# A transformer block on one core: another schedule for the row maxima of its softmax

## The chip, the cores and the metric

The kernel runs on 1 core of one Trainium2 chip. The metric is device time in microseconds (us) per execution, the median of several runs.

The engines are named as the profile names them: PE (TensorE; PEld is its weight load), DVE (VectorE), ACT (ScalarE), POOL (GpSimd), SP (SyncE, which here mostly issues DMAs).

## The reference

One transformer block with adaptive LayerNorm over a sequence of S = 2048 rows and D = 448 columns, 16 heads of 28, F = 1792:

```python
mod = (_silu(c) @ w_mod).reshape(c.shape[0], 6, 1, -1)
sa, ca, ga, sb, cb, gb = (mod[:, 0], mod[:, 1], mod[:, 2], mod[:, 3], mod[:, 4], mod[:, 5])
h = _layernorm(x, axis=-1) * (1 + ca) + sa
x = x + ga * _A_ref(h, A_wqkv, A_wo)             # softmax attention, 16 heads
h = _layernorm(x, axis=-1) * (1 + cb) + sb
x = x + gb * _B_ref(h, B_w1, B_b1, B_w2, B_b2)   # LayerNorm, dense, gelu, dense
```

In the attention, `p = _softmax(scores)` over 2048 keys for each of 16 x 2048 query rows, `o = p @ v`, and the heads' outputs times `wo`. The change touches the softmax alone.

## The kernel before

Matmuls that need precision are split in a high and a low part in a one-pass format (hi·hi + lo·hi + hi·lo, the "three terms"). The program has three stages: projections to queries, keys and values; the attention loop; the MLP.

**The attention loop.** Heads lie four to a group g (four groups), 32 partitions apart, so a group fills 128 partitions. Queries are cut in four blocks qt of 512. One *unit* u is one (g, qt), 16 units; one *step* is 128 keys of a unit, 16 steps kt per unit, 256 in all. A step makes, for two *halves* hf of two heads each, the scores [128 keys, 2 heads, 512 queries] by 3 terms x 2 matmuls into a two-bank tile in PSUM, then ACT's exponential of the whole tile (L1167). Behind both halves stands the product with V of the step before (L1132, `av`), which fills all 128 rows of the PE array, where a score matmul fills 28 or 29. Row sums come out of a column of ones in V.

**The row maxima.** The exponential needs the row maximum subtracted. It is taken from the high parts alone, ahead of time: for a unit (g, qt), each of 4 chunks cch of 512 keys, 4 row blocks i and 4 heads j, one matmul [128 queries, 512 keys] (`max_mm`, L466) into a one-bank tile, and one DVE reduction of 512 to 1 (`max_one`, L471): 64 per unit, 1024 in all. When a unit's 64 are counted, `max_fin` reduces and transposes them, and small DMAs put them into the query tile `qst` as a further row, so that the score matmul subtracts them. The maxima of unit u+1 must therefore be done before its first step. `mxq` is the queue of maxima that may be made; `emit_max` takes one from it, `finish_max` forces the rest of a unit.

In the projection stage some maxima are made in *pairs* already (`pair_diff`): with k1 - k0 as key, ACT's relu of the scores' difference, then DVE adds q·k0 to it and takes the maximum in one operation (L483), since max(a, b) = a + relu(b - a).

Of the 1024 maxima 884 single ones are made in the loop or near it: four in an even step, three in an odd one, until they run out in unit 14 (`n_maxima`).

**Tiles in PSUM.** Eight banks: two score tiles `s0`, `s1` of two banks, a bank `o` for the product with V, and three banks for maxima (`m1`, and `m2` with two buffers). When no maxima are left, `third_tile` closes `m2` and opens a third score tile `s2` in its place. A tile is written again only when its last reader is done.

**Other work in the loop.** `sched` holds functions by step: the end of a unit (`unit_end_tasks`: denominators by DMA, reciprocal on DVE, product on POOL, a cast on DVE), the output projection (`t_wo`, steps 8 to 11 of units 12 to 15, "projection steps", with `load_o` as its loads), the second LayerNorm of block 0 (`ln2_stages`), weight preparation. The order of every engine's instructions is that in which the code emits them.

Of the kernel before, what the change touches and what calls it, by code (L numbers as in the profile page):

```python
# [27 lines left out]
NB = S // 512  # L28
# [4 lines left out]
P1RATE = 4  # L33
YTAGS = [f"{a}{i}" for a in ("kh", "qh") for i in range(4)]
# [5 lines left out]
def tile_adaln_block(ctx: ExitStack, tc: tile.TileContext, x, wqkv, wo, w1, b1, w2, b2, c, w_mod, out):  # L40
# [42 lines left out]
    def slot4(tag, inner, dt=F32R):  # L83
        if tag not in halved:
            t = slot(tag, [128, 4] + inner, dt)
            return lambda k: t[:, k]
        t2 = [slot(tag + h, [128, 2] + inner, dt) for h in ("", "h")]
        return lambda k: t2[k // 2][:, k % 2]

    def ps_s2():  # L90
        s_ring.append(s_ring.pop(0))
        key = s_ring[-1]
        return ps_pools[key][1].tile([128, 2, 512], F32, tag=key, name=nm(key), bufs=1)
# [365 lines left out]
    def max_mm(g, qt, i, j, k, ps=None):  # L459
        if (g, qt) not in mxp:  # L460
            mxp[(g, qt)] = sbt("mxp", [128, 4, 4, 4], bufs=6)
            if (g, qt) in paired:
                pool.memset(mxp[(g, qt)][:, :, :, 0:1], -3.0e38)
# [25 lines left out]

    def load_hi(kind, g, b):  # L490
        tg = ("kh" if kind else "qh") + str(b)
        t = sb.tile([128, 512], F32R, tag=tg, name=nm(tg), bufs=1)
        (kh_sb if kind else qh_sb)[(g, b)] = t
        sp.dma_start(f(t), f(dscr[kind][0][g])[:, b * 512 : (b + 1) * 512])

# [67 lines left out]
    last_j = [None]  # L563

    def emit_max(n, half=None):
        for _ in range(n):
            if not mxq:
                return
            fits = [x for x, m in enumerate(mxq[:32]) if half is None or (m[4] // 2 == half and m[4] != last_j[0])]
            g, qt, cch, i, j = mxq.pop(fits[0] if fits else 0)  # L570
            last_j[0] = j
            max_one(g, qt, cch, i, j)
            count(g, qt, [cch])

# [35 lines left out]
    def finish_max(g, qt):  # L610
        while left[(g, qt)] > 0:
# [185 lines left out]
    s_ring[:] = ["s1", "s0"]  # L797
    mx_ring[:] = ["m1", "m2", "m2"]

    def third_tile(on):  # L800
        ps_close("m2" if on else "s2")
        ps_open("s2" if on else "m2", "right")
        s_ring[:] = s_ring + ["s2"] if on else ["s1", "s0"]
        mx_ring[:] = ["m1"] if on else ["m1", "m2", "m2"]

    phase1[0] = False
    for item in deferred:
# [63 lines left out]
    def unit_end_tasks(u, o_sb):  # L871
# [62 lines left out]
        if len(parts) > 1 and not staged:  # L934
            tasks.append((0, lambda: load_o(qt)))
# [136 lines left out]

    for i in range(5):
# [7 lines left out]
    for i in range(14):  # L1081
        at(last0 - 12 + i, lambda i=i: lnst[0][0](i))
    for k in range(NC):
        at(last0 + 3 + k, lambda k=k: lnst[0][1](k))
# [23 lines left out]
    plain = [0]  # L1108
# [6 lines left out]
    def left_steps(s_):  # L1115
        rest = range(s_, NKT * (NU - 1) - 6)
        n_wo = sum(is_wo(x) for x in rest)
        return len(rest) - n_wo, n_wo


    def n_maxima(s_):
        n_plain, n_wo = left_steps(s_)
        over = len(mxq) - 7 * n_plain // 2
# [173 lines left out]
```

## Time and profile before

| | |
|---|---|
| median of 3 runs | 1128.31 us (1128.06 to 1128.99) |
| the profiled execution | 1130.08 us, span 1128.0 us |
| granted PE clock | 1.0 of full speed |
| the attention loop, from the first exponential of step 0 to that of step 255 | 170.26 to 830.90 us |
| busy: PE, DVE, ACT, POOL | 1116.4, 843.7, 672.0, 209.6 us |
| DVE's maxima in the loop (L471 from `m`) | 884, 568.8 us, 686 ns each |
| exponentials (L1167), 512 | 1019 to 1025 ns each |

The profile is of one execution on this core. The timeline gives start and duration of instructions on each engine, in brackets the idle time before one and what released it; consecutive like ones are merged with a count. The windows give busy time and counts of instructions in a stretch, the groups the mean duration by line and shape. Matmuls are pipelined, and four of them on different rows of the array can run at once, so the sum of their durations is larger than the time that passes.

### The profile page before, as it was taken

What the parts mean: (1) busy time and instruction counts of PE and PEld (TensorE: products, weight loads), DVE (VectorE), ACT (ScalarE), POOL (GpSimd) and SP (SyncE); (2) the same over time, 40 slices, a digit from 0 to 9 for tenths busy, and PEclk for the clock granted to TensorE, in tenths of its full rate; (3) what the DMA queues carried; (4) which work ended last, traced back from release to release, by engine and by line L of the source; (5) the groups of instructions that cost most, each with busy time, mean ns of one, the idle gap of its engine ahead of it and who ended that gap; (6) DMA issues with size and microseconds to landing.
All of it is one profiled execution on the core that took longest, in us unless ns stands there. A gap on an engine that the chain in (4) does not pass through costs nothing.

```text
span 1128.0 us, 20665 instructions
## 1 busy us (share of the span) xinstructions
PE 1116.4 (99%) x8319; PEld 670.1 (59%) x8319; DVE 843.7 (75%) x1485; ACT 672.0 (60%) x823; POOL 209.6 (19%) x211
## 2 busy tenths in 40 slices
PE   8999999999999999999999999999999999999998
PEld 6756674444444444444444454545468888888887
DVE  6968788999999999999999978595448853444322
ACT  4555657888887888788788867576752321111110
POOL 1533332110000000000000020217114504123000
PEclk9999999999999999999999999999999999999999
DMA  9562263121121211311111312020422100000000
GB/s 303 202 200 88 91 200 114 48 84 41 58 95 57 58 40 57 91 53 58 53 44 58 112 41 83 4 85 1 137 73 78 35 33 1 1 33 1 33 1 33
DMA packets 49341, 81.19 MB, mean 72 GB/s; under 512 B 12311, under 2 KB 18702, under 8 KB 49234
## 3 DMA queue, kind: packets, MB, share of 16 engines
q1 hardware_dynamic: 48762, 79.14, 22.1%
q8 instruction: 65, 1.06, 0.4%
q10 hardware_dynamic: 148, 0.46, 0.1%
q0 software_dynamic: 336, 0.28, 0.1%
q14 instruction: 30, 0.25, 0.1%
HBM read 55.04 MB, written 26.48 MB: 72 GB/s over the span
## 4 chain that ended last, share of the span: by engine, by line
PE 94%; DVE 3%; ACT 1%; DMA 1%; issue 1%; POOL 0%; SPq 0%; DVEq 0%; ACTq 0%; POOLq 0%
PE s L1162 26%; PE o L1132 22%; PE m L386 16%; PE pa L386 8%; PE m L466 6%; PE s L1232 3%; PE s L1233 3%; PE s L1231 3%; DVE mxp L471 2%; PE t L1232 1%; PE t L1233 1%; PE t L1231 1%; DMA slot_c<-in_w_mod_dram 1%; PE ma L466 1%; PE o L267 1%
## 5 line engine op out<-in xcount | busy, mean ns | idle before, releaser
L471 DVE TENSOR_REDUCE mxp<-m 128x1 f32<-128x512 f32 x884 | 568.8, 686 | 75.3 <-PE m L466 41.1
L1162 PE MATMUL s<-slot_b,slot_a 28*128 28x512 f32 (+1 forms) x3072 | 376.3, 420 | 0.0
L1162 PEld LDWEIGHTS s<-slot_b,slot_a 28*128 28x128 f32 (+1 forms) x3072 | 213.0, 184 | 247.4 <-ACT slot_c L1167 124.1
L466 PE MATMUL m<-kh,qh 28*128 28x512 f32 x863 | 287.6, 472 | 1.2 <-DVE mxp L471 0.9
L1167 ACT ACTIVATE slot_c<-s 128x1024 f32<-128x1024 f32 x170 | 174.3, 1025 | 75.9 <-PE s L1162 75.6
L1132 PE MATMUL o<-slot_c,v 128*32 128x512 f32 x680 | 178.8, 605 | 0.0
L1208 ACT ACTIVATE full<-m,b_col 128x512 f32<-128x512 f32 x56 | 38.6, 689 | 192.0 <-PE m L386 175.5
L1132 PE MATMUL o<-slot_c1h,v 128*32 128x512 f32 x512 | 134.7, 605 | 0.0
L1132 PE MATMUL o<-slot_c0h,v 128*32 128x512 f32 x512 | 134.7, 605 | 0.0
L1167 ACT ACTIVATE slot_c0h<-s 128x1024 f32<-128x1024 f32 x128 | 130.4, 1019 | 2.4 <-PE m L386 2.4
L1167 ACT ACTIVATE slot_c1h<-s 128x1024 f32<-128x1024 f32 x128 | 130.4, 1019 | 0.0
L1211 DVE CAST hi<-full 128x512 fp32r<-128x512 f32 x56 | 25.5, 455 | 134.6 <-ACT full L1208 134.6
L466 PEld LDWEIGHTS m<-kh,qh 28*128 28x128 f32 x863 | 114.3, 182 | 8.6 <-DVE mxp L471 5.1
L1167 ACT ACTIVATE slot_d<-s 128x1024 f32<-128x1024 f32 x86 | 88.1, 1025 | 39.3 <-PE s L1162 39.1
L895 POOL TENSOR_TENSOR osb<-osb,osb 128x512 f32<-128x512 f32 x16 | 20.9, 1307 | 441.1 <-DMA osb<-drec 356.8
L1132 PE MATMUL o<-slot_d,v 128*32 128x512 f32 x344 | 90.5, 605 | 0.4 <-ACT osb L1101 0.4
L386 PE MATMUL m<-y,slot_a 128*128 128x512 f32 x160 | 60.7, 395 | 0.0
L1132 PEld LDWEIGHTS o<-slot_c,v 128*32 128x32 f32 x680 | 24.5, 108 | 52.4 <-issue 49.5
L1212 DVE TENSOR_TENSOR lo<-full,hi 128x512 fp32r<-128x512 f32 x56 | 44.2, 788 | 5.9 <-DVE hi L1211 0.9
L471 DVE TENSOR_REDUCE mxp<-ma 128x1 f32<-128x512 f32 x54 | 35.6, 683 | 7.1 <-PE m L466 4.8
L386 PE MATMUL m<-y,slot_v 128*128 128x512 f32 x112 | 39.2, 396 | 0.0
L386 PE MATMUL m<-y,slot_b 128*128 128x512 f32 x112 | 39.0, 398 | 0.0
(316 smaller groups left out, 1626.7 us busy)
## 6 DMA issues: line engine op xcount, KB each, us to landing
slot_b<-d SPq DMA_DIRECT2D x32, 256.0 KB
slot_a<-d SPq DMA_DIRECT2D x32, 256.0 KB
d<-lo SPq DMA_DIRECT2D x28, 256.0 KB
d<-hi SPq DMA_DIRECT2D x16, 256.0 KB
osb<-drec SPq DMA_DIRECT2D x15, 256.0 KB
out_dram<-xn SPq DMA_DIRECT2D x16, 224.0 KB
raw<-in_B_w_dram SPq DMA_DIRECT2D x14, 224.0 KB
qh<-d SPq DMA_DIRECT2D x12, 256.0 KB
```

What stands on the lines that cost most here:

```text
L386: pe.matmul(p, a, b, start=(i == 0), stop=(i == len(terms) - 1))
L466: pe.matmul(m, qh_sb[(g, qt)][js, i * 128 : (i + 1) * 128], k[js, :], start=True, stop=True)
L471: dve.tensor_reduce(out=mxp[(g, qt)][:, i, j, cch : cch + 1], in_=m, op=ALU.max, axis=AX.X)
L1132: pe.matmul(o[32 * j : 32 * j + 32, :], v_sb[kt // 4][:, kt % 4, 4 * g + j, :], p[j // 2][:, j % 2, :], start=(kt == 0), stop=(kt == NKT - 1),
L1162: pe.matmul(s2[:, jj, :], ks[rows_, kp, kc], qs[rows_, qp, :], start=(term == 0), stop=(term == 2))
L1167: act.activation(pt[hf], s2, AF.Exp, scale=SCALE)
L1208: act.activation(gf, p, AF.Gelu_apprx_tanh, bias=b1_col[:, i : i + 1])
L1211: dve.tensor_copy(ghi, gf)
L1212: dve.tensor_tensor(out=glo, in0=gf, in1=f(ghi), op=ALU.subtract)
L1231: pe.matmul(pp, ghi[:, ts], w_hi, start=(m == 0), stop=False)
L1232: pe.matmul(pp, ghi[:, ts], w_lo, start=False, stop=False)
L1233: pe.matmul(pp, glo[:, ts], w_hi, start=False, stop=(m == NFT - 1))
```

## The change

Three things are changed in the order of the maxima, and a few tasks are moved.

1. Up to step 118 one pair of maxima every two steps is made in two steps, as in the projection stage. `make_kd` has POOL subtract two key chunks; at the end of an odd step, behind the product with V, `open_pair` emits the max matmul of the difference and ACT's relu; in the next odd step `close_pair` emits the second matmul and DVE's add-and-max in the place of one single maximum. An odd step so covers four maxima with three DVE operations.
2. From step 119 (`RING`), outside the projection steps, three score tiles are open (`s0`, `s1`, `s2`) and one bank `m1` for maxima. A step's first half is in `s0`, its second half in `s1` or `s2` by turns, and the third tile holds two maxima of neighbouring heads, which one DVE reduction of 2 x 512 to 2 takes (`emit_pair`); a single one goes to `m1`. Three maxima per step, with one more where `extra` finds it due. The half that comes first alternates by step.
3. In projection steps three maxima are made, in the old tiles.

Moved: the queries of the next unit are loaded in step 4 instead of 1, `load_o` four steps earlier, the second LayerNorm of block 0 three steps later, `finish_max` from step 10 to 12 of a unit. The maxima of all units are first set to a low value on POOL.

The counts of the built program: in the loop before, 884 single reductions; now 564 single ones, 55 pairs by relu and 105 wide reductions (564 + 110 + 210 = 884). Up to step 118 every step covers four maxima but a few (none in steps 28 and 29); from step 119 to 234 every step makes three, `extra` is never used, and the last maxima stand in step 235, before in step 233.

The diff, cut to what the text speaks of:

```diff
+LAST_MAX = NKT - 4
+RING = 119
+PAIR_AT = (2, 2, 0, 2)
+WO_MAX = 3
...
+def make_kd(g):
+    c0 = PAIR_AT[g]
+    kd.update(g=g, t=slot("d0h", [128, 1, 512]), **{"from": clock[0] + 1})
+    pool.tensor_tensor(out=kd["t"][:, 0, :], in0=f(kh_sb[(g, c0 + 1)]), in1=f(kh_sb[(g, c0)]), op=ALU.subtract)
...
+def open_pair():
...
+            p = max_mm(g, qt, i, j, kd["t"][:, 0, :])
+            r = slot("d0i", [128, 1, 512], F32)[:, 0, :]
+            act.activation(r, p, AF.Relu)
+            px_open.append((m, r))
...
+def close_pair():
+    (g, qt, cch, i, j), r = px_open.pop()
+    p = max_mm(g, qt, i, j, kh_sb[(g, cch)])
+    dve.tensor_tensor_reduce(
+        out=r, in0=p, in1=r, scale=1.0, scalar=-3.0e38, op0=ALU.add, op1=ALU.max,
+        accum_out=mxp[(g, qt)][:, i, j, cch + 1 : cch + 2],
+    )
+    count(g, qt, [cch, cch + 1])
...
+def emit_pair(half, t):
...
+            for jj in range(2):
+                max_mm(g, qt, i, j + jj, kh_sb[(g, cch)], lambda: t[:, jj])
+            dve.tensor_reduce(out=mxp[(g, qt)][:, i, j : j + 2, cch], in_=t, op=ALU.max, axis=AX.X)
...
-            if kt == 1 and u + 1 < NU and u + 1 not in qst:
+            if kt == 4 and u + 1 < NU and u + 1 not in qst:
                 load_q(u + 1)
-            if kt == NKT - 6 and u + 1 < NU:
+            clock[0] = step
+            if kt == LAST_MAX and u + 1 < NU:
                 finish_max(*divmod(u + 1, NB))
...
-            n = n_maxima(step)
-            n0 = 1 if n == 3 and step % 4 == 3 else 2
+            now[0] = turns[step % 2]
+            first = step % 2 if step >= RING else 0
+            pt = {hf: slot(tags[step % len(tags)], [128, 2, 512], F32) for hf, tags in zip((first, 1 - first), ptags)}
+            was, ring = ring, step >= RING and (three or not is_wo(step))
+            if ring != was:
+                third_tile(ring)
+            more = ring and not three and extra(step)
+            late_one, after = after, more
+            n_max = 0 if ring else WO_MAX if is_wo(step) else 4 - step % 2
+            n0 = 1 if step % 4 == 3 else 2
+            closing = bool(px_open) and step % 2 == 1
...
-            for hf in range(2):
-                s2 = ps_s2()
+            for n, hf in enumerate((first, 1 - first)):
+                s2 = ps_s2() if three else ps_two((now[0] if n else "s0") if ring else ("s0", "s1")[n])
                 for term, (kp, qp) in enumerate(((0, 0), (1, 0), (0, 1))):
+                    if ring and n == 1 and term == 2 and mxq:
+                        emit_pair(first, ps_two(turns[1 - step % 2]))
                     for jj in range(2):
                         rows_ = slice(64 * hf + 32 * jj, 64 * hf + 32 * jj + DH + (term == 0))
                         pe.matmul(s2[:, jj, :], ks[rows_, kp, kc], qs[rows_, qp, :], start=(term == 0), stop=(term == 2))
-                    if hf == 0 and term < min(n0, n):
-                        emit_max(1, 1)
-                    if hf == 1 and term == 2 and n > n0:
-                        emit_max(n - n0, 0)
+                    if closing:
+                        if (n, term) == (0, 0):
+                            close_pair()
+                    elif n == 0 and term < n0 <= n_max:
+                        emit_single(1, ps_mx)
+                    if n == 1 and term == 2:
+                        for _ in range(2 if closing else n_max - n0):
+                            emit_single(0, ps_mx)
+                    if ring and (n, term) == ((1, 0) if late_one else (0, 0)) and not three:
+                        emit_single(1 - first, ps_mx)
+                    if n == 1 and term == 2 and more:
+                        emit_single(first, ps_mx)
                 act.activation(pt[hf], s2, AF.Exp, scale=SCALE)
...
+            if step % 2 and step + 2 < RING:
+                open_pair()
```

How the order of instructions moves is seen best in single steps. PE, step 182 of the loop (unit 11, step 6), before: score matmuls L1162 into `s1` and `s0`, maxima L466 into the `m` tiles, the product with V L1132 into `o`.

```order
L1162 MATMUL s1_2022_8436<-slot_b1_1846_7704,slot_a1_1500_6273 128x512 x2
L466 MATMUL m2_2023_8439<-kh0_1717_7166,qh1_1522_6358 128x512
L1162 MATMUL s1_2022_8436<-slot_b1_1846_7704,slot_a1_1500_6273 128x512 x2
L466 MATMUL m2_2024_8444<-kh1_1757_7331,qh1_1522_6358 128x512
L1162 MATMUL s1_2022_8436<-slot_b1_1846_7704,slot_a1_1500_6273 128x512 x2
L1162 MATMUL s0_2025_8450<-slot_b1_1846_7704,slot_a1_1500_6273 128x512 x6
L466 MATMUL m1_2026_8457<-kh1_1757_7331,qh1_1522_6358 128x512
L466 MATMUL m2_2027_8460<-kh1_1757_7331,qh1_1522_6358 128x512
L1132 MATMUL o_1975_8250<-slot_c0_2011_8398,v1_229 32x512 x2
L1132 MATMUL o_1975_8250<-slot_c1h_2012_8399,v1_229 32x512 x2
```

The same step in the changed program, where score matmuls are L1287, maxima L474 and the product L1245:

```order
L1287 MATMUL s0_2034_8434<-slot_b1_1908_7862,slot_a1_1606_6486 128x512 x2
L474 MATMUL m1_2035_8437<-kh2_1797_7352,qh1_1634_6608 128x512
L1287 MATMUL s0_2034_8434<-slot_b1_1908_7862,slot_a1_1606_6486 128x512 x4
L1287 MATMUL s1_2036_8445<-slot_b1_1908_7862,slot_a1_1606_6486 128x512 x4
L474 MATMUL s2_2037_8450<-kh1_1757_7171,qh1_1634_6608 128x512 x2
L1287 MATMUL s1_2036_8445<-slot_b1_1908_7862,slot_a1_1606_6486 128x512 x2
L1245 MATMUL o_1995_8267<-slot_c1h_2025_8399,v1_230 32x512 x2
L1245 MATMUL o_1995_8267<-slot_c0_2024_8398,v1_230 32x512 x2
```

Four maxima have become three, two of them in one two-bank tile `s2`, ahead of the last two score matmuls; in step 183 `s1` and `s2` change places.

ACT in steps 86 to 88, before: the exponentials alone.

```order
L1167 ACTIVATE slot_c1_1220_5100<-s1_1222_5102 128x1024
L1167 ACTIVATE slot_c0h_1221_5101<-s0_1228_5123 128x1024
L1167 ACTIVATE slot_d0_1231_5141<-s1_1233_5143 128x1024
L1167 ACTIVATE slot_c1h_1232_5142<-s0_1235_5154 128x1024
L1167 ACTIVATE slot_c0_1238_5172<-s1_1240_5174 128x1024
L1167 ACTIVATE slot_c0h_1239_5173<-s0_1243_5188 128x1024
```

The same steps in the changed program, with the exponentials at L1300 and the relu at L631:

```order
L1300 ACTIVATE slot_c1_1295_5246<-s0_1297_5248 128x1024
L1300 ACTIVATE slot_c0h_1296_5247<-s1_1300_5262 128x1024
L1300 ACTIVATE slot_d0_1303_5280<-s0_1305_5282 128x1024
L1300 ACTIVATE slot_c1h_1304_5281<-s1_1307_5293 128x1024
L631 ACTIVATE slot_d0i_1311_5313<-m1_1310_5311 128x512
L1300 ACTIVATE slot_c0_1312_5315<-s0_1314_5317 128x1024
L1300 ACTIVATE slot_c0h_1313_5316<-s1_1317_5331 128x1024
```

The relu of tile `m1_1310` stands between the odd step's second exponential and the even step's first one.

More of the change, by code (lines that the diff above doesn't have):

```diff
@@ L796, in tile_adaln_block @@
         ps_open(key)
[L797 to L798 removed]
+    turns = ("s1", "s2")
     def third_tile(on):
@@ L1107, in tile_adaln_block @@
     o = None
-    plain = [0]
+    due = [0.0]
+    now = [None]
     three = False
@@ L1137, in tile_adaln_block @@
     ptags = (["d0", "c0", "c1"], ["c0h", "c1h"])
-    done_max = set()
+    after = False
+    ring = False
     for u in range(NU):
```

128 lines of the change are left out of this document (101 added, 27 removed).

## The prediction

> **What bounds the kernel now.** I read first the page's engine rows, then one stretch of the attention loop by engine, then two steps of it instruction by instruction, and last the groups for durations.
>
> ```profile
> PE 1116.4 (99%) x8319; PEld 670.1 (59%) x8319; DVE 843.7 (75%) x1485; ACT 672.0 (60%) x823; POOL 209.6 (19%) x211
> ```
>
> PE is called 99% busy, but a busy PE may be waiting in the middle of its pipeline, so this row decides nothing. The windows of the exponentials (two per step) give the pace; the columns are length, busy time and count:
>
> ```profile
> 212.60:464.82 252.22, 199.75 (x206) 1.00 0.20 62
> 464.82:643.07 178.25, 141.59 (x146) 1.00 0.21 64
> 779.19:787.14 7.95, 7.65 (x8) 1.00 0.01 2
> 212.60:464.82 252.22, 252.22 (x2428) 112.90 (x2428) 236.61 (x389) 203.64 (x213) 16.80 (x19) 1.00 0.20 62
> ```
>
> Steps 16 to 118 take 252.22 / 103 = 2.449 us each, steps 119 to 191 178.25 / 73 = 2.442. The third row is steps 236 to 239, where no maxima are left and a third score tile is open: 1.99 each. The fourth row is all engines over the first window (PE, PEld, DVE, ACT, POOL): DVE is busy 236.61 / 51.5 = 4.59 us of every two steps of 4.89, so it is close, but not full. What sets 4.89 shows in the timeline of two steps, an even one with four maxima and an odd one with three (start, duration):
>
> ```profile
> 402.12 1.02 ACT L1167 ACTIVATE slot_c1h<-s 128x1024 f32<-128x1024 f32 x1
> 403.36 1.02 ACT L1167 ACTIVATE slot_c<-s 128x1024 f32<-128x1024 f32 x1 [0.23 <-PE s L1162]
> 404.28 1.02 ACT L1167 ACTIVATE slot_c0h<-s 128x1024 f32<-128x1024 f32 x1
> 406.09 1.02 ACT L1167 ACTIVATE slot_c<-s 128x1024 f32<-128x1024 f32 x1 [0.80 <-PE s L1162]
> 407.01 1.02 ACT L1167 ACTIVATE slot_c1h<-s 128x1024 f32<-128x1024 f32 x1
> ```
>
> ```profile
> 402.35 0.50 PE L1162 MATMUL s<-slot_b,slot_a 29*128 29x512 f32 x2
> 402.69 0.99 PE L1162 MATMUL s<-slot_b,slot_a 28*128 28x512 f32 x6
> 403.18 0.18 PEld L1162 LDWEIGHTS s<-slot_b,slot_a 29*128 29x128 f32 x2 [0.31 <-ACT slot_c1h L1167]
> 403.21 0.50 PE L466 MATMUL m<-kh,qh 28*128 28x512 f32 x1
> 403.52 0.39 PE L1162 MATMUL s<-slot_b,slot_a 28*128 28x512 f32 x2
> 403.75 0.40 PE L1162 MATMUL s<-slot_b,slot_a 28*128 28x512 f32 x2
> 404.09 0.62 PE L1132 MATMUL o<-slot_d,v 128*32 128x512 f32 x2
> 405.09 0.50 PE L1162 MATMUL s<-slot_b,slot_a 29*128 29x512 f32 x2
> 405.35 0.74 PE L1162 MATMUL s<-slot_b,slot_a 29*128 29x512 f32 x8
> 405.89 0.40 PE L466 MATMUL m<-kh,qh 28*128 28x512 f32 x2
> 406.25 0.62 PE L1132 MATMUL o<-slot_c,v 128*32 128x512 f32 x2
> 407.25 0.50 PE L1162 MATMUL s<-slot_b,slot_a 29*128 29x512 f32 x2
> 402.93 4.76 DVE L471 TENSOR_REDUCE mxp<-m 128x1 f32<-128x512 f32 x7 [0.28 <-PE m L466]
> ```
>
> Read it as a ring of waits. The odd step's second exponential starts at 402.12 and ends at 403.14. Only then is its score tile free, and the even step's second half loads weights at 403.18 (0.31 of waiting, released by ACT). From there 0.91 to the product with V at 404.09, 1.00 to the odd step's first score at 405.09, 1.00 to its first exponential at 406.09, 0.92 to its second at 407.01: 407.01 - 402.12 = 4.89, the period. No maximum is on this ring. Two score tiles set it, and maxima ride along as long as DVE's 4.59 fits.
>
> **The change, part by part.** Durations that the terms use:
>
> ```profile
> L471 DVE TENSOR_REDUCE mxp<-m 128x1 f32<-128x512 f32 x884 | 568.8, 686 | 75.3 <-PE m L466 41.1 <-PE ma L466 8.4 <-PE s L1162 4.2
> L502 DVE TENSOR_REDUCE m<-mxp 128x16 fp32r<-128x64 f32 x16 | 3.5, 220 | 0.6
> L1167 ACT ACTIVATE slot_c1h<-s 128x1024 f32<-128x1024 f32 x128 | 130.4, 1019 | 0.0
> L479 ACT ACTIVATE slot_d0h<-m 128x512 f32<-128x512 f32 x23 | 13.3, 597 | 20.4 <-PE m L466 11.5 <-PE ma L466 7.6 <-PE o L466 1.4
> L483 DVE CUSTOM_DVE_ANT_0 slot_d0h<-m,slot_d0h 128x512 f32<-128x512 f32 x8 | 5.5, 682 | 0.0
> L483 DVE DVE_READ_ACCUMULATOR2_ANT mxp<- 128x1 f32 x39 | 3.2, 83 | 0.0
> L905 DVE CAST hi<-osb 128x512 fp32r<-128x512 f32 x15 | 6.3, 417 | 3.7 <-POOL osb L895 3.7
> L886 DVE RECIPROCAL den<-den 128x16 f32<-128x16 f32 x16 | 3.9, 244 | 4.3 <-DMA den<-osb 4.3
> L509 DVE STREAM_TRANSPOSE full<-m 128x32 f32<-128x32 f32 x16 | 3.2, 203 | 0.1
> L429 POOL TENSOR_TENSOR lo<-full,hi 128x512 fp32r<-128x512 f32 x16 | 20.6, 1286 | 33.2 <-ACT hi L425 15.3 <-issue 12.5 <-DVE hi L425 4.0
> ```
>
> *Three score tiles, step 119 on, 105 plain steps.* The ring above is cut: a step's second half no longer waits for the exponential of the step before, but for the wide reduce, which read that tile. Count from a step's first score. The single reduce starts 0.58 later (402.93 - 402.35) and takes 0.69: 1.27. The wide matmuls can start at 0.80 (405.89 - 405.09) and end 0.40 later, so the wide reduce starts at 1.27, behind the single one. Its duration no row shows: 448 more elements cost 686 - 220 = 466 ns, 1.04 ns each, so 512 more make it 1.22. From below, ACT's step from 512 to 1024 (597 to 1019) adds 0.42: 1.11; from above, twice the narrow one: 1.37. I take 1.22, from the same engine and operation. Then 1.27 + 1.22 = 2.49, 0.04 to the waiting second half, 0.91 to the product, 1.00 to the step after next: 4.44 for two steps, 2.22 each. Behind the waiting score stand the wide matmuls of that step and the product with V, so all of PE waits. The floor is the odd step of today, 407.25 - 405.09 = 2.16: it holds the same PE work, twelve score matmuls and three maxima, with no wait. By the bounds of the wide reduce a step takes 2.16 to 2.30; ACT needs about 2 x 0.92 plus a tail and fits. Term: 105 x (2.442 - 2.22) = -23.3, bounds -29.6 to -14.9.
>
> This needs PE to start the second half's scores while the first half's still run. In the rows it does: the odd step's next scores start at 405.35, 0.26 after the first, and the maximum at 403.21 starts ahead of scores at 403.52 that stand before it in program order. The Trainium skill, page "PSUM — Partial Sum Buffer", section "Engine vs sequencer instructions", says that matmuls start and complete in program order; by that rule the ring step would be no shorter than today's. The trace disagrees here (403.21 before 403.52), so it stays a rival with a small chance.
>
> *The pair by relu, 55 times up to step 118.* Each adds a max matmul behind the product in the odd step, a relu on ACT, and 0.083 of accumulator read; the fused add-and-max (682 ns) takes the place of a reduce (686). DVE's seven operations per two steps now cover eight maxima; the ones saved let the later stage run at three per step. The relu waits for its matmul, which starts with the even step, and both exponentials of that step queue behind it. New ring: matmul 0.50, relu 0.50 (597 less the 0.10 by which exponentials overlap, 1.02 against 0.92), exponentials 0.92 + 1.02, 0.04 to PE, 0.91 to the product, 1.00 to the next even step: 4.89, as long as the old one, with nothing to spare. DVE beside it: 4.59 + 0.08 = 4.67 by today's overlap; without overlap 7 x 0.686 + 0.083 + a unit's other work (417 + 244 + 220 + 203 = 1.08 us in 8 pairs of steps, 0.14) = 5.02. So 0 to +0.13; I take +0.08, nearer DVE's end, since two full rings must now hold at once. A gain is excluded, since the ring of two score tiles stays. From above, if the relu lies on the ring whole: +0.60. Term: 55 x 0.08 = +4.4, likely bounds 0 to +7.2. Two steps without any maxima (28, 29) gain nothing for the same reason.
>
> *Moved work.* Query loads three steps later, output loads four steps earlier (two to six DMAs on SP's queue, which still have 12 steps or 24 us), block 0's second LayerNorm three steps later, and on POOL whole memsets and four subtracts of 1.29: POOL is busy 16.80 of 252.22. The last unit's maxima end at step 235 instead of 233, still ahead of that unit's start at 240, about 8 us at 1.99 a step. Opening and closing the third tile around the projection steps may cost a few tenths, six times; the LayerNorm's shift may give as much. All taken as 0, bounds -2.6 to +3. If SP's or POOL's cover fails, one unit waits once for some 1.3 to 3 us. Projection steps keep their three maxima.
>
> Sum: -23.3 + 4.4 + 0 = -18.9. Against the profiled execution's 1130.08 (span 1128.0) that is 1111.2; the median of the timed runs, 1128.31, is 1.8 lower, and the sum is taken from it: **1109.4**.
>
> **The rivals.**
>
> *A, PE's floor.* The wide reduce is cheap, the relu free: -29.6, so 1098.7. For: DVE's reduces partly overlap today. Against: the relu's ring is as long as 4.89, and DVE's end longer.
>
> *B, DVE paces both stages.* The wide reduce costs 1.37 (a step of 2.30) and unit-end work lands between the reduces, 1.08 in 16 steps, half of it felt: 2.33, so 105 x 0.112 = -11.8; pairs at 5.02, +7.2: -4.6, 1123.7. For: DVE at 94% in the windows. Against: in the ring stage it needs 0.69 + 1.22 = 1.91 of 2.22. With a little more of each this reaches no change.
>
> *C, slower: the relu on the ring whole.* ACT is in order, and the tile that the relu reads comes free only after it; the third maximum behind it waits for that tile, then the product. If both exponentials of the odd step shift by 0.60, pairs cost 5.49: 55 x 0.60 = +33.0, with -23.3 it is +9.7, 1138.0. It turns the sign where a pair of steps costs over 4.89 + 23.3 / 55 = 5.31. Against: ACT waits 0.23 and 0.80 in a pair of steps, more than the relu's 0.50.
>
> *D, slower: strict order on PE.* The ring's second half starts only after the first's third score, 0.34 + 0.23 = 0.57 in (402.69 - 402.35, 403.75 - 403.52), then 0.91 and 1.00: 2.48 per step, 105 x 0.04 = +4.0, with +4.4: 1136.7. Against: the rows named above. Such an order is what the Trainium skill states, page "PSUM — Partial Sum Buffer", section "Engine vs sequencer instructions".
>
> **How the numbers follow.** Forecast 0.62 (its own range 1100 to 1121), A 0.06, B 0.17, C 0.11, D 0.04. About 0.2%, 2.3 us, is what a measurement of this kernel can tell from no change. Faster: 0.62 + 0.06 + 0.12 of B = 0.80; within: the other 0.05 of B; slower: C and D, 0.15. The range takes in the forecast and B with small additions, 1100 to 1126, and leaves out A, C and D, 0.21.
>
> **What would show it.** In the profile after: exponentials in the ring stage 2.2 us per pair, score weights in their second half waiting for DVE and not for ACT; wide reduces of 1.22; steps 16 to 118 at 2.45 to 2.52 each, relus of 0.6 ahead of the even step's exponentials. The forecast is wrong if ring steps stay above 2.35, if even and odd step before step 119 take over 5.1 together, or if PE's scores of a step no longer overlap.

## The result, and the profile after

The changed kernel takes **1126.53 us** (median of 20 runs, 1124.64 to 1128.93) against 1128.64 for the kernel before (20 runs): a ratio of 0.9978, 95% interval 0.9972 to 0.9984. It is faster by 2.1 us, where 18.9 were forecast and the range ended at 1126. The profiled execution took 1128.93 (span 1127.2), the longest of the 20 and 2.4 above their median; that of the kernel before was 1.4 above its own. So the stages below, read from the two traces, add up to -0.8 and not to -2.1.

The engine rows of the page and the groups of the three kinds of maxima (partitions x elements and count, then busy time and mean ns of one, then the idle time before them):

```profile
PE 1113.3 (99%) x8319; PEld 675.3 (60%) x8319; DVE 803.6 (71%) x1380; ACT 695.2 (62%) x878; POOL 216.5 (19%) x228
L479 DVE TENSOR_REDUCE mxp<-m 128x1 f32<-128x512 f32 x564 | 364.2, 685 | 97.7 <-PE m L474 68.0
L674 DVE TENSOR_REDUCE mxp<-s 128x2 f32<-128x1024 f32 x105 | 128.6, 1225 | 4.2 <-PE s L474 0.2
L638 DVE CUSTOM_DVE_ANT_0 slot_d0i<-m,slot_d0i 128x512 f32<-128x512 f32 x55 | 38.0, 690 | 15.7 <-PE m L474 11.4
```

The wide reduce takes 1225 ns, as estimated (1.22), and DVE does 40 us less. The windows of the exponentials over steps 0 to 118 in the kernel before (its steps 119 to 191 stand in the prediction), and over steps 0 to 118 and 119 to 191 in the changed one:

```profile
170.26:464.82 294.56, 230.88 (x238) 1.00 0.21 64
```

```profile
174.14:481.24 307.10, 231.28 (x239) 1.00 0.20 60
481.24:646.44 165.20, 141.87 (x146) 1.00 0.26 76
```

The borders and lengths give an account by stage (us):

| stage | before | after | difference | forecast |
|---|---|---|---|---|
| up to the loop's first exponential | 170.3 | 174.1 | +3.9 | 0 |
| steps 0 to 118 (pairs) | 294.6 | 307.1 | +12.5 | +4.4 |
| steps 119 to 191 (three tiles) | 178.3 | 165.2 | -13.0 | -16.2 |
| steps 192 to 239 (32 plain ones) | 144.1 | 141.2 | -2.9 | -7.1 |
| from step 240 on | 340.8 | 339.5 | -1.3 | 0 |

Four stages are over the forecast: the one before the loop, the pairs, the three tiles, and the steps from 192 on with the projection steps. Their causes were read from the trace and then tried by experiment. The -1.3 of the last stage lies in unit 15 up to step 255 (43.8 us before, 42.5 after); its cause was not tried.

**Before the loop** a memset is waited for. POOL, then DVE, of the changed kernel (start, duration, in brackets the idle time before and what ended it):

```profile
31.25 1.29 POOL L438 TENSOR_TENSOR lo<-full,kh 128x512 fp32r<-128x512 f32 x1
32.50 1.29 POOL L438 TENSOR_TENSOR lo<-full,raw 128x512 fp32r<-128x512 f32 x1
33.72 0.16 POOL L471 MEMSET mxp<- 128x64 f32 x1
```

```profile
33.91 1.29 DVE L479 TENSOR_REDUCE mxp<-ma 128x1 f32<-128x512 f32 x2 [3.76 <-POOL mxp L471]
```

In the changed kernel the tile that receives the first maxima is set low first. The memset takes 0.16, but it is issued with the first max matmul, behind POOL's splits, so the first reduce waits 3.76 and holds the PSUM tile that TensorE needs next.

**In unit 12** (steps 199 and 200) there is a stall of 3.04 + 7.05 us where the steps around take 2.3 to 4.4. SyncE's issues, POOL and DVE of the changed kernel there:

```profile
652.79 0.32 SPq L996 DMA_DIRECT2D drec<-den  x1
655.48 0.54 SPq L998 DMA_DIRECT2D osb<-drec  x1
656.07 0.94 SPq L760 DMA_DIRECT2D slot_b<-d  x2
```

```profile
662.15 1.28 POOL L1003 TENSOR_TENSOR osb<-osb,osb 128x512 f32<-128x512 f32 x1 [25.80 <-DMA osb<-drec]
```

```profile
663.46 0.43 DVE L1013 CAST hi<-osb 128x512 fp32r<-128x512 f32 x1 [2.02 <-POOL osb L1003]
663.80 0.68 DVE L479 TENSOR_REDUCE mxp<-m 128x1 f32<-128x512 f32 x1
```

The small `osb` load issued at 655.48 lands at 662, with the moved query load right behind it. DVE stands at the cast of that unit, with the maxima behind it in its queue, and TensorE waits for those. Behind this wait the granted clock of this execution fell, as these windows show (PE, PEld, DVE, ACT, POOL, then clock, DMA share and GB/s):

```profile
664.00:668.00 4.00, 3.07 (x21) 0.98 (x21) 3.50 (x5) 2.27 (x3) 1.24 (x1) 0.79 0.03 6
668.00:672.00 4.00, 4.00 (x28) 2.91 (x24) 0.10 (x1) 0.53 (x1) 0.14 (x1) 0.78 0.00 0
```

Over step 200 it is 0.76, so some 1.7 of its 7.05 us (0.24 x 7.05) are the slower clock.

### The profile page after: what moved, and what is told of

Same layout as the page of the kernel before. It is cut to its first block, busy times and chain, and to the rows that moved or that the text cites. A ratio compares the mean times of both kernels' runs of the same rounds, so it can differ in the third digit from the quotient of the medians.

```text
span 1127.2 us, 20699 instructions
## 1 busy us (share of the span) xinstructions
PE 1113.3 (99%) x8319; PEld 675.3 (60%) x8319; DVE 803.6 (71%) x1380; ACT 695.2 (62%) x878; POOL 216.5 (19%) x228
## 4 chain that ended last, share of the span: by engine, by line
PE 86%; DVE 2%; ACT 1%; DMA 1%; issue 1%; POOL 0%; SPq 0%; DVEq 0%; POOLq 0%; ACTq 0%
PE s L1287 21%; PE o L1245 21%; PE m L395 16%; PE m L474 7%; PE pa L395 5%; PE s L1367 3%; PE s L1368 3%; PE s L1366 3%; PE s L474 1%; PE t L1367 1%; PE t L1368 1%; PE t L1366 1%; DVE mxp L479 1%; DMA osb<-drec 1%; PE m L276 1%
## 5 line engine op out<-in xcount | busy, mean ns | idle before, releaser
L479 DVE TENSOR_REDUCE mxp<-m 128x1 f32<-128x512 f32 x564 | 364.2, 685 | 97.7 <-PE m L474 68.0
L1287 PE MATMUL s<-slot_b,slot_a 28*128 28x512 f32 (+1 forms) x3072 | 355.3, 424 | 1.7 <-DVE mxp L674 0.8
L1287 PEld LDWEIGHTS s<-slot_b,slot_a 28*128 28x128 f32 (+1 forms) x3072 | 211.1, 183 | 172.0 <-ACT slot_c L1300 93.3
L474 PE MATMUL m<-kh,qh 28*128 28x512 f32 x598 | 221.0, 462 | 2.3 <-DVE mxp L479 0.6
L1300 ACT ACTIVATE slot_c<-s 128x1024 f32<-128x1024 f32 x170 | 174.6, 1027 | 55.7 <-PE s L1287 52.4
L1245 PE MATMUL o<-slot_c,v 128*32 128x512 f32 x680 | 179.7, 607 | 0.0
L1245 PE MATMUL o<-slot_c1h,v 128*32 128x512 f32 x512 | 135.5, 608 | 0.9 <-ACT slot_c1h L1300 0.9
L1245 PE MATMUL o<-slot_c0h,v 128*32 128x512 f32 x512 | 134.7, 605 | 0.0
L1300 ACT ACTIVATE slot_c0h<-s 128x1024 f32<-128x1024 f32 x128 | 131.3, 1026 | 3.3 <-PE m L395 2.4
L674 DVE TENSOR_REDUCE mxp<-s 128x2 f32<-128x1024 f32 x105 | 128.6, 1225 | 4.2 <-PE s L474 0.2
L1300 ACT ACTIVATE slot_c1h<-s 128x1024 f32<-128x1024 f32 x128 | 130.7, 1021 | 0.0
L1300 ACT ACTIVATE slot_d<-s 128x1024 f32<-128x1024 f32 x86 | 88.3, 1027 | 30.0 <-PE s L1287 28.4
L474 PEld LDWEIGHTS m<-kh,qh 28*128 28x128 f32 x598 | 92.4, 182 | 20.0 <-DVE mxp L479 12.0
L1245 PE MATMUL o<-slot_d,v 128*32 128x512 f32 x344 | 90.5, 605 | 0.4 <-ACT osb L1209 0.4
L638 DVE CUSTOM_DVE_ANT_0 slot_d0i<-m,slot_d0i 128x512 f32<-128x512 f32 x55 | 38.0, 690 | 15.7 <-PE m L474 11.4
L1245 PEld LDWEIGHTS o<-slot_c,v 128*32 128x32 f32 x680 | 24.5, 108 | 38.1 <-issue 36.3
L474 PE MATMUL s<-kh,qh 28*128 28x512 f32 x210 | 46.5, 438 | 0.0
```

Source lines behind the costliest of these rows:

```text
L474: pe.matmul(m, qh_sb[(g, qt)][js, i * 128 : (i + 1) * 128], k[js, :], start=True, stop=True)
L479: dve.tensor_reduce(out=mxp[(g, qt)][:, i, j, cch : cch + 1], in_=m, op=ALU.max, axis=AX.X)
L674: dve.tensor_reduce(out=mxp[(g, qt)][:, i, j : j + 2, cch], in_=t, op=ALU.max, axis=AX.X)
L1245: pe.matmul(o[32 * j : 32 * j + 32, :], v_sb[kt // 4][:, kt % 4, 4 * g + j, :], p[j // 2][:, j % 2, :], start=(kt == 0), stop=(kt == NKT - 1),
L1287: pe.matmul(s2[:, jj, :], ks[rows_, kp, kc], qs[rows_, qp, :], start=(term == 0), stop=(term == 2))
L1300: act.activation(pt[hf], s2, AF.Exp, scale=SCALE)
```

## The experiments

Each ratio is to the kernel before, timed beside the run.

**Memset only where it is needed.** Maxima that are all written by reductions need no low value; only the units made partly by pairs keep the memset.

```diff
+PAIRED = ((0, 1), (0, 2), (0, 3), (1, 0), (1, 1), (1, 2), (2, 0), (2, 1), (2, 2), (2, 3))
...
-            pool.memset(mxp[(g, qt)], -3.0e38)
+            if (g, qt) in PAIRED:
+                pool.memset(mxp[(g, qt)], -3.0e38)
```

> The changed kernel, but POOL sets only those units' maxima to a low value in which a pair by relu is closed. Theory (the changed kernel loses 3.9 us ahead of the loop and some in step 171, because the first reduce of a unit waits for a memset that stands behind longer work on POOL): the 3.8 us wait of DVE for POOL near 33 us goes and the loop starts about 2.3 us earlier, the pause near 600 us goes too (about 1.4): 3 to 4 us less than the changed kernel, about 1123. Rival (the pause is taken up later, or the loop's start was late for another reason): under 1 us.

Measured 1122.52 us, ratio 0.9942 (0.9930 to 0.9955). DVE of this kernel:

```profile
30.07 1.29 DVE L481 TENSOR_REDUCE mxp<-ma 128x1 f32<-128x512 f32 x2 [0.74 <-PE m L476]
```

The wait of 3.76 is 0.74 again, the loop starts at 170.8 (after: 174.1), and unit 10, where a memset stood behind a split in the middle of the loop, goes from 37.25 to 35.87. The memset cost about 4 us, shown.

**Query load back to step 1 of a unit.**

```diff
-            if kt == 4 and u + 1 < NU and u + 1 not in qst:
+            if kt == 1 and u + 1 < NU and u + 1 not in qst:
```

> The changed kernel with the next unit's queries loaded in step 1 of a unit again and not in step 4. Theory (in unit 12 the load sits right behind the broadcast of the reciprocals on SP's queue and shares the DMA engines with it, 6.5 us for it where it took 5.0 before, and DVE waits in order for the product on POOL): step 200 falls from 7.05 to about 5, the clock stays at full speed there, 2 to 3.5 us less, about 1123.5. Rival (the steps are shorter, so the same chain is too long whatever shares the DMA engines): step 200 stays over 6, under 1 us.

Measured 1125.86, ratio 0.9976 (0.9968 to 0.9985), not to be told from the change's 0.9978. In its trace step 200 takes 4.83 and not 7.05. Three other kernels with the load still in step 4 show 5.25, 5.39 and 5.50 there, at a full clock, and all eight with three tiles and the load in step 1 show 4.80 to 4.83. So the load costs some half a microsecond in that step, by the traces; the larger part of what step 200 took more was the clock of one execution, and the expected 2 to 3.5 us are not there.

**The single maxima on their half of the rows.** `emit_single` chooses a maximum for a half of the rows that the score matmuls of that moment leave free. Up to step 118 its key puts `x in kept` (not one of those kept for pairs) ahead of the half. Counted in the program, 53 single maxima so go to the half in which the scores are running. The same order lets two maxima in a row use the same head, that is the same rows, 18 times in odd steps; the kernel before passed over the head that it had just used (`last_j`).

```diff
-            m = min(near, key=lambda x: (x in kept, x[4] // 2 != half, x[4] in js))
+            m = min(near, key=lambda x: (x[4] // 2 != half, x in kept, x[4] in js))
```

> The changed kernel, but a single maximum is chosen from the asked half first and only then spared for a pair (53 of the single maxima before step 119 lay in the other half, in units 1, 2, 4 and 5; now none; still 55 pairs). Theory (such a matmul stands on the rows of the scores that run, and so lengthens the step): units 4 and 5 fall from 41.8 and 42.8 to about 40.2 us, unit 1 by 1, together 5 to 6 us, about 1121. Rival (units 1, 4 and 5 are longer because of waits for loads or because of the tile ring): under 1.5 us.

Measured 1120.25, ratio 0.9922 (0.9909 to 0.9936): 6.3 us of gain from the order of three terms. The window of steps 0 to 118:

```profile
174.17:475.20 301.03, 231.63 (x239) 1.00 0.21 63
```

That is 301.0 against 307.1, with as many maxima and pairs as before. The edit leaves none of the 53 and none of the 18, so the choice of maxima cost the 6.07 us as a whole; 6.07 / 53 = 0.11 us for each wrong half is a mean that holds both.

**No pairs.** The call of `open_pair` is taken out; the rest of the change stays, so the maxima that the pairs no longer make fall to the three-tile stage.

```diff
-            if step % 2 and step + 2 < RING:
-                open_pair()
```

> The changed kernel without pairs by relu in the loop: four and three maxima up to step 118 as before, and from step 119 three or four, since 54 more are left. Theory (a pair costs 0.13 us per two steps and more by its choice of heads; a fourth maximum in a three-tile step costs about 0.5): steps 16 to 118 back to 2.445 each, the fourth maxima add 50 x 0.5 = 25 us: about 1140, slower than the changed kernel by some 13. Rival (a fourth maximum is nearly free in a three-tile step): 1115 or less.

Measured 1163.17, ratio 1.0302 (1.0288 to 1.0316), far over the expected 1140. The window of steps 119 to 191:

```profile
477.59:670.61 193.02, 141.88 (x146) 1.00 0.22 66
```

It takes 193.0 and not 165.2: most steps with a fourth maximum take some 2.74, and step 219, with nine forced ones behind it, 9.08. The three-tile stage pays with three maxima and not with four.

The first stage of this run shows what else the choice of maxima costs, for it has no pairs and should have taken the 294.6 us of the kernel before:

```profile
174.68:477.59 302.91, 231.01 (x239) 1.00 0.20 60
```

Counted in the program, 36 of its singles go to the wrong half and 21 in odd steps to the head just used. Take an even step and the odd one behind it, from step 16 to 117. Of 19 such twos without a wrong half or a repeated head, 17 take 4.88 to 4.91, as in the kernel before. Eleven have no wrong half but the same head twice in a row in the odd step, and take 5.08 to 5.33. So a repeated head in the odd step costs some 0.2 or more by itself, and without either fault and without pairs the new code costs nothing extra.

**Pairs alone.** From step 119 the two tiles of before stay.

```diff
-RING = 119
+RING = 10**6
...
-        for m in pairable() if clock[0] < RING else ():
+        for m in pairable() if clock[0] < 119 else ():
...
-            was, ring = ring, step >= RING and (three or not is_wo(step))
+            was, ring = ring, three
...
-            if step % 2 and step + 2 < RING:
+            if step % 2 and step + 2 < 119:
```

> The changed kernel with the first part of the change alone: the 55 pairs by relu up to step 118 stay, and from step 119 the two score tiles of the kernel before stay, with four and three maxima by turns, until the maxima run out (step 220). Theory (a pair moves maxima forward and saves nothing by itself): start of the loop and steps 0 to 118 as in the changed kernel, 174.1 and 307.1 us, so 16.4 above the kernel before; steps 119 to 191 as before, 178.3; the third score tile opens some 13 steps earlier, worth 13 x (2.44 - 1.99) = -5.9, so about 1139. Rival (the saved reduces are a gain of their own): at or below 1129.

Measured 1140.5, ratio 1.0103 (1.0087 to 1.0118). Steps 119 to 191 take 178.25, to the hundredth as before, and the maxima that end earlier give back 3.8 in steps 192 to 239. Of the 11.7 us over the kernel before some 10 are the memset and the choice of maxima, which this run still holds. By this subtraction neither half of the change gains by itself, even without these faults: the pairs are the price of a stage with three maxima a step.

**The three repairs together.** Memset, query load and half as above (the pair set with (1, 3) besides).

> The three repairs together: memsets only where pairs are closed, queries loaded in step 1, singles from the asked half. Theory (three separate losses): the sum of their single gains, 4.0 + 0.7 + 6.3 = 11.0 below the changed kernel's 1126.5: 1115.5, within 2. Rival (they share one loss, such as the start's late clock): 1118 or more.

Measured **1116.08** (1114.63 to 1116.95), ratio 0.9880 (0.9864 to 0.9897), faster than both kernels. The next five runs start from it and ask what sets the two rates that are left; in four of them parts of the maxima are left out, and the exponent's scale is lowered so that nothing overflows. Its windows:

```profile
170.76:473.39 302.63, 231.60 (x238) 0.99 0.21 62
473.39:637.16 163.77, 141.77 (x146) 1.00 0.25 75
```

**The pairs without the relu.** ACT does nothing for them; POOL sets the relu's tile to zero, so the larger of two chunks is not taken.

```diff
-            act.activation(r, p, AF.Relu)
+            pool.memset(r, 0.0)
```

> The kernel with the three repairs, but ACT makes no relu: POOL sets that tile to zero instead, so the maxima of the pairs are not those of the reference, and the exponentials' scale is made a hundredth so that they can't overflow. Theory (relu and the tile that it holds are what lengthens two steps from 4.89 to about 5.0): steps 0 to 118, 301 us with the relu, fall to about 295. Rival (DVE's seven operations and the accumulator read set it): 300 or more.

Measured 1115.26, ratio 0.9877 (0.9855 to 0.9899). The plain units 3, 5 and 6 take 40.07, 39.85 and 39.73 in place of 40.05, 39.96 and 39.96: 0.01 us per pair. The relu is not on the ring. (This run and the next two were timed twice each.)

**Single reduces over half a tile, up to step 118.**

```diff
-        dve.tensor_reduce(out=mxp[(g, qt)][:, i, j, cch : cch + 1], in_=m, op=ALU.max, axis=AX.X)
+        n = 512 if phase1[0] or clock[0] >= RING else 256
+        dve.tensor_reduce(out=mxp[(g, qt)][:, i, j, cch : cch + 1], in_=m[:, :n], op=ALU.max, axis=AX.X)
```

> The kernel with the three repairs, but single maxima up to step 118 are taken over 256 of 512 scores (not the reference's maxima; exponentials' scale a hundredth). PE and ACT do the same work, DVE's six reductions in two steps take about 0.42 instead of 0.69. Theory (relu's ring): steps 0 to 118 stay within 1.5 us of 301. Rival (DVE sets the pace): they fall to about 295.

Measured 1109.52, ratio 0.9827 (0.9807 to 0.9846). Its window of steps 0 to 118:

```profile
170.94:465.92 294.98, 231.40 (x238) 1.00 0.22 64
```

With relu and pairs in place the steps take 295.0, against 294.6 in the kernel before; units 3, 5 and 6 are 39.29, 39.42 and 39.26, where two tiles without pairs gave 39.13. So DVE is what the pairs pay for, 0.08 of the 0.11 us that a pair costs. The repeated head seems not to add to it: in the repaired kernel nearly all even steps to 118 still have one, but the three twos of steps from 34 to 111 without one take 4.98 to 5.08, no less than the others.

**The wide reduce over 2 x 256**, so 0.69 us and not 1.23.

```diff
-                dve.tensor_reduce(out=mxp[(g, qt)][:, i, j : j + 2, cch], in_=t, op=ALU.max, axis=AX.X)
+                dve.tensor_reduce(out=mxp[(g, qt)][:, i, j : j + 2, cch], in_=t[:, :, :256], op=ALU.max, axis=AX.X)
```

> The kernel with the three repairs, but the wide reduction from step 119 on reads 2 x 256 of 2 x 512 scores (not the reference's maxima; exponentials' scale a hundredth): 0.69 instead of 1.225 us. Theory (a ring step waits for the wide reduction): steps 119 to 191 fall from 163.8 us to about 73 x 2.16 = 157.7. Rival (PE or ACT sets 2.245): over 162.

Measured 1112.3, ratio 0.9851 (0.9831 to 0.9871). The group of the wide reduces and the window of steps 119 to 191:

```profile
L676 DVE TENSOR_REDUCE mxp<-s 128x2 f32<-128x512 f32 x105 | 72.7, 693 | 6.6 <-PE s L1289 0.3
471.21:633.27 162.06, 141.78 (x146) 1.00 0.25 76
```

The stage gives back 1.7 us of 163.8, although DVE is free for half a microsecond more in each step. In the repaired kernel the wide reduce is on the ring. DVE and then TensorE of the repaired kernel, over two steps:

```profile
561.20 1.23 DVE L676 TENSOR_REDUCE mxp<-s 128x2 f32<-128x1024 f32 x1
562.68 0.69 DVE L481 TENSOR_REDUCE mxp<-m 128x1 f32<-128x512 f32 x1 [0.26 <-PE s L1289]
563.36 1.23 DVE L676 TENSOR_REDUCE mxp<-s 128x2 f32<-128x1024 f32 x1
564.95 0.69 DVE L481 TENSOR_REDUCE mxp<-m 128x1 f32<-128x512 f32 x1 [0.37 <-PE m L476]
565.65 1.23 DVE L676 TENSOR_REDUCE mxp<-s 128x2 f32<-128x1024 f32 x1
```

```profile
562.45 0.77 PE L1289 MATMUL s<-slot_b,slot_a 28*128 28x512 f32 x8
563.38 0.62 PE L1247 MATMUL o<-slot_c,v 128*32 128x512 f32 x2
564.38 0.50 PE L1289 MATMUL s<-slot_b,slot_a 29*128 29x512 f32 x2
564.64 0.73 PE L1289 MATMUL s<-slot_b,slot_a 29*128 29x512 f32 x8
```

The wide reduce ends at 562.43 and the waiting second half starts at 562.45; 0.93 to the product, 1.00 to the next scores, 0.57 and 0.70 to the next wide reduce at 565.65: 4.45 from wide reduce to wide reduce, the forecast's ring. With the short reduce another ring of the same length is left. TensorE's weight loads and ACT of the run with the short reduce:

```profile
559.84 0.18 PEld L476 LDWEIGHTS s<-kh,qh 28*128 28x128 f32 x2 [0.19 <-ACT slot_c0h L1302]
560.28 0.11 PEld L1247 LDWEIGHTS o<-slot_c,v 128*32 128x32 f32 x2 [0.24 <-issue]
561.27 0.18 PEld L1289 LDWEIGHTS s<-slot_b,slot_a 29*128 29x128 f32 x2 [0.84 <-ACT slot_d L1302]
564.27 0.19 PEld L476 LDWEIGHTS s<-kh,qh 28*128 28x128 f32 x2 [0.19 <-ACT slot_c0h L1302]
```

```profile
562.28 1.02 ACT L1302 ACTIVATE slot_c<-s 128x1024 f32<-128x1024 f32 x1 [0.21 <-PE s L1289]
563.20 1.02 ACT L1302 ACTIVATE slot_c0h<-s 128x1024 f32<-128x1024 f32 x1
```

The wide max matmuls write the tile whose exponential (`slot_c0h`) has just ended. From there 0.44 to the product, 0.99 to the next scores, 1.01 to the first exponential, 0.92 to the second, 1.02 until it ends, 0.05 to the next such load: 564.27 - 559.84 = 4.43. In this run nearly every two steps take 4.42 to 4.48; in the repaired kernel about two of three do and the third takes 4.51 to 4.59, it seems where the two rings meet.

**Max matmuls of the wide tile over 256 columns too.**

```diff
-        pe.matmul(m, qh_sb[(g, qt)][js, i * 128 : (i + 1) * 128], k[js, :], start=True, stop=True)
+        n = m.shape[-1]
+        pe.matmul(m, qh_sb[(g, qt)][js, i * 128 : (i + 1) * 128], k[js, :n], start=True, stop=True)
...
-                    max_mm(g, qt, i, j + jj, kh_sb[(g, cch)], lambda: t[:, jj])
+                    max_mm(g, qt, i, j + jj, kh_sb[(g, cch)], lambda: t[:, jj, :256])
```

> The repaired kernel with the wide reduce over 2 x 256, as in the run before, and with both matmuls of a wide tile over 256 columns too (the upper halves of the keys' maxima are left out, the exponent's scale is lowered so that nothing overflows). With the narrower reduce alone steps 119 to 191 went from 163.8 to 162.1. If TensorE's own work sets the ring step: two max matmuls of half the length take about 0.05 to 0.09 us off each step (a step with three maxima is 2.24, one with none 1.99: 0.08 for one max matmul), steps 119 to 191 near 157 and the total near 1104. If the ring is set by the exponentials and the tile that they free: steps 119 to 191 stay at 162, total 1112.

Measured 1113.13, ratio 0.9858 (0.9842 to 0.9875). The window of steps 119 to 191:

```profile
472.73:634.70 161.97, 141.75 (x146) 1.00 0.25 76
```

It takes 161.97 against 162.06. Less work for TensorE changes nothing, so the max matmuls' work does not set this step. The ring through the exponentials is what the trace leaves; no run shortened an exponential to show it.

**Wide max matmuls behind the last scores.**

```diff
                 for term, (kp, qp) in enumerate(((0, 0), (1, 0), (0, 1))):
-                    if ring and n == 1 and term == 2 and mxq:
-                        emit_pair(first, ps_two(turns[1 - step % 2]))
                     for jj in range(2):
...
+                    if ring and n == 1 and term == 2 and mxq:
+                        emit_pair(first, ps_two(turns[1 - step % 2]))
```

> The repaired kernel with the two wide max matmuls behind the last score matmuls of the step, not ahead of them. They wait for the second exponential of the step before (0.15 us in half of the steps), and the last two score matmuls wait behind them. If that wait is on the ring, the second exponential starts earlier and steps 119 to 191 fall by up to 73 x 0.07 = 5 us, total 1111. If TensorE's work alone sets the step, the order makes no difference: 163.8 and 1116. If the wide reduce, now later, holds up the tile: slower than 1116.

Measured 1125.02, ratio 0.9965 (0.9952 to 0.9978). The window of steps 119 to 191 and the group of the wide reduces in this kernel:

```profile
472.11:642.22 170.11, 141.59 (x147) 1.00 0.24 72
L676 DVE TENSOR_REDUCE mxp<-s 128x2 f32<-128x1024 f32 x105 | 128.7, 1226 | 22.5 <-PE s L1287 22.2
```

A step takes 2.33. The wide reduces now wait 0.2 each for TensorE, and every two steps take 4.63 to 4.68: 0.2 more on the ring of the wide reduce is 0.2 more in two steps. That this ring sets the pace when it is the longer one is shown.

**First pair of key group 2 two steps later.** In the repaired kernel TensorE waits for the subtract of the keys. POOL and TensorE there, and then the windows of the stretch (PE, PEld, DVE, ACT, POOL, then the granted clock and DMA):

```profile
360.37 1.29 POOL L1016 TENSOR_TENSOR lo<-osb,hi 128x512 fp32r<-128x512 f32 x1 [4.12 <-DVE hi L1015]
361.61 1.27 POOL L601 TENSOR_TENSOR slot_d0h<-kh,kh 128x512 fp32r<-128x512 f32 x1
362.94 0.49 PE L476 MATMUL m<-slot_d0h,qh 28*128 28x512 f32 x1 [1.04 <-POOL slot_d0h L601]
```

```profile
361.00:363.00 2.00, 0.96 (x12) 0.06 (x4) 1.27 (x4) 1.58 (x2) 2.00 (x5) 1.00 0.59 223
363.00:365.00 2.00, 2.00 (x21) 1.38 (x25) 1.46 (x3) 1.53 (x3) 0.10 (x2) 0.94 0.12 43
365.00:367.00 2.00, 2.00 (x12) 0.42 (x8) 1.03 (x2) 0.90 (x1) 0.00 (x0) 0.50 0.00 0
367.00:369.00 2.00, 2.00 (x23) 0.95 (x19) 1.14 (x3) 0.73 (x1) 0.00 (x0) 0.71 0.00 0
```

```diff
-        kd.update(g=g, t=slot("d0h", [128, 1, 512]), **{"from": clock[0] + 1})
+        kd.update(g=g, t=slot("d0h", [128, 1, 512]), **{"from": clock[0] + (3 if g == 2 else 1)})
```

> The repaired kernel with the first pair of key group 2 opened two steps later. In the repaired kernel TensorE waits 1.04 us in step 75 for GpSimd's subtract of the two key chunks, which stands behind another subtract of 1.29; step 75 takes 3.32, and in some executions the clock falls to half behind it and step 76 takes 4.31 instead of 2.74. One pair fewer fits (54), and the last maxima stand in step 236 instead of 235. Theory: step 75 near 2.2, step 76 at 2.74, so -1.1, or -2.7 against an execution with the fall, +0.2 for step 236: 1114 to 1115 against 1116.1. Rival (another wait takes its place): 1116 or more.

Measured 1116.51 (1115.92 to 1116.65), ratio 0.9886 (0.9869 to 0.9902): no gain. The wait is gone (step 75 takes 2.20, step 76 2.74, steps 0 to 118 299.6 against 302.6), but unit 7 takes 39.17 and not 38.04, and steps 192 to 239 0.6 more. With a pair fewer the later stages give it back. Unit 7's loss stands in two steps behind the opening of the third tile: steps 123 and 124 take 2.50 and 3.26 against 2.23 and 2.22, and TensorE waits there for wide reduces; why they are late was not tried.

## Why the prediction was wrong, point by point

**What bounds the kernel: right.** The ring of two score tiles governed the pairs' stage too: with DVE relieved, it returned to 39.3 per unit against 39.13.

**Two steps failed, both terms put at nothing. The first is "Moved work ... All taken as 0".** "Whole memsets" were priced by POOL's load in the middle of the loop (16.80 of 252.22 busy). The place that decides is the projection stage, where POOL's splits stand in a row and the first reduce waits for the memset behind them: 3.4 us there (a loop start of 174.1 against 170.8), 1.4 in unit 10, about 4.0 in the medians. The text had the sentence "If SP's or POOL's cover fails, one unit waits once for some 1.3 to 3 us" and did not ask in which unit the first user comes. Here the memset was covered or not at its first user, not on average.

**The second, and the larger, is the stage up to step 118, whose only term was the pairs' +4.4: which single maximum is taken had no term at all.** The key of `emit_single` stands in the new code; its order sends 53 matmuls to the wrong half of the rows and, 18 times in odd steps, one to the head just used: 6.1 us together. Counts of maxima per step were the same, so an account by counts could not see it. The stage took +12.5.

**The pair's term, +0.08 each: near.** Measured on the repaired kernel's plain units, (39.99 - 39.13) / 8 = 0.11, of which DVE is most; 55 of them make about 6 against 4.4, within the bounds of 0 to 7.2. Steps 16 to 118 take (307.10 - 42.43) / 103 = 2.57 in the changed kernel, over the 2.45 to 2.52 that were to show, and two of them 5.14, over the 5.1 that was named as a sign of being wrong; with the choice of maxima put right it is 2.51. The repaired kernel is still 8.1 over the kernel before in steps 0 to 118: some 6 are the pairs, and the rest is mainly the one wait in step 75 with the clock's fall behind it.

**The three-tile step, 2.22: right in mechanism, 0.02 short.** In the repaired kernel it is 163.8 / 73 = 2.243. The forecast's ring of 4.44 for two steps is there at 4.43 to 4.45, and the wide reduce is as estimated. The ring through the third tile's exponential, as long, was not seen; about 0.12 is added in every third pair of steps, which goes with the short reduce. Over 105 steps 0.023 each are 2.5 us. The floor called "2.16, the same PE work" does not bind: with half of the wide tile's columns in the max matmuls nothing moved.

**The steps from 192 on gave -2.9 in place of -7.1.** The stall in unit 12 accounts for some 2.3 of it, of which some 1.7 are the clock in that one execution (the stage takes 138.9 with the memset repaired, 138.5 with all repairs). The rest would be the ring's 0.02 and the closing and opening of the third tile, which no run measured by itself.

**The rivals.** A (PE's floor) has no support: no stage runs at 2.16 a step, and fewer columns for the max matmuls gain nothing. B came nearest in size, 1123.7, but only its pair of steps (5.02, measured 5.00) is there; its ring step of 2.33 is not. C is refuted: without the relu next to nothing changes, and with the choice of maxima put right a pair of steps takes 5.00, under 5.31. D is refuted: the ring step is 2.243, under 2.48 and under the two-tile step. The matmul order that D took from the Trainium skill, page "PSUM — Partial Sum Buffer", section "Engine vs sequencer instructions" (matmuls start and complete in program order) does not agree with the trace: the maximum at 403.21 starts ahead of scores at 403.52 that stand before it.

**The account.** The forecast was 1109.4, the changed kernel takes 1126.53, and 10.4 of the difference go with the repairs: the memset (4.0), the choice of maxima (6.3) and the query load's small share. That the change is faster at all, as forecast, is because these faults cost less than the third tile gains. The repaired kernel should then have met the forecast and takes 1116.08. The 6.7 that remain are put down to the ring (2.5), the pairs (1 to 1.6), the subtract's wait in step 75 (1.0 to 2.6, though without it nothing was gained) and the edges of the projection steps; the last is what is left over and was not measured.

## What to carry to other kernels

Price a moved or added small operation at its first user: find what stands ahead of it in its queue there, since an average share of busy time says nothing about one place. When code chooses among equal pieces of work, check the choice and not only the count: here pieces on rows of the array that were in use, or had just been used, were dearer. Before pricing the removal of a ring, look for the other rings that pass through the same buffers; here two of nearly equal length lost a little more than either shows.

## What the runs showed of the hardware

A pause of TensorE of 1.04 us was followed by a granted clock of 0.50 for about 3.4 us (worked out from 0.94, 0.50 and 0.71 in the windows above), and step 76 took 4.31 us and not 2.74. Whether it falls differs: four other kernels whose step 75 takes 3.30 to 3.32 with the same wait have 2.74 to 2.77 in step 76, a fifth has 4.22. The changed kernel kept its clock behind the memset's wait and lost it in step 200; with the query load in step 1 it lost it behind the memset's wait (0.80 from 30 to 38 us). The Trainium skill, page "TensorE: Matmul & The Clock Gate", section "What's actually happening", says that the clock falls after at least one idle window of about 3.4 us; the length of the slow stretch agrees with such a window, the pause of 1.04 us before it was shorter. One reduction of 2 x 512 took 1225 ns where two of 512 take 1370, and one of 2 x 256 took 693, as one of 512 does (685): DVE paid mostly by elements here, and little for the second output.
